# Attention in units of four heads: block transposes on VectorE, scores on four 32-row tiles, and the weights of six experts loaded late

## The chip, the cores and the metric

The kernel runs on one core of a Trainium2 chip. The metric is the device time of one execution in microseconds (us). It was taken several times for each kernel; a time is called fast when it is within 1.5% of the fastest of the same kernel. Only fast runs are compared, and all ratios are fast runs against fast runs of the kernel before, run in turn on the same chip.

Names used below: PE is TensorE, PEld its weight loads, DVE is VectorE, ACT is ScalarE, POOL is GpSimd, SP is SyncE (here it only issues DMAs). AV is the product of the attention weights with v, and the granted clock is the share of its full clock that TensorE was allowed. L307 is line 307 of the kernel in question, so line numbers differ between kernels.

## The reference

Attention for 4 batches, 8 heads, 768 positions and 64 dimensions, with a distance bias and a mask that keeps the first 8 positions and the 96 most recent ones. Its 3072 output rows (512 wide) then go through a mixture of 8 experts: the gate scores of all tokens are sorted, and tokens are handed out so that each expert gets exactly 384. Each expert is two matrix products with a ReLU between.

```python
def _attn_ref(q, k, v, n_global, n_local):          # q, k, v: (4, 8, 768, 64) fp32
    scores = np.matmul(q, k.transpose(0, 1, 3, 2)) / np.sqrt(D)
    is_global = pos[None, :] < n_global             # 8
    is_local = (rel >= 0) & (rel < n_local)         # 96
    ...
    scores = np.where(is_global | is_local, scores + bias[None], -1e9)
    a = softmax(scores)                             # cut
    return np.matmul(a, v)

def _moe_ref(x, w_gate, w1, w2):                    # x: (3072, 512), 8 experts, 1024 hidden
    order = np.argsort(-(x @ w_gate).flatten())
    ...                                             # greedy, at most 384 tokens each
    for e in range(E):
        out[assigned == e] = np.maximum(x[assigned == e] @ w1[e], 0.0) @ w2[e]
```

## The kernel before

The kernel has three stages, one after the other: attention, routing (which ends with the indices `idi`, saying which token goes to which expert), and the experts, which gather their rows from `x_tok` in DRAM by those indices.

Attention works on pairs of heads. q and k are loaded with six consecutive tokens to a partition, GpSimd reorders them, TensorE transposes them in blocks of 128, VectorE and ScalarE copy the results out. The scores of a pair take 14 matmuls of 64 rows (a head's 64 dimensions), two of them side by side in the array. The trace lists each fp32 score matmul as two records (28 a pair), here called half-passes.

```python
def reorder(n, dst, srcs):                                    # GpSimd
    nc.gpsimd.tensor_copy(out=dst.rearrange("p j t d -> p t j d"), in_=srcs[n % NR])

def kT(n, hf):                                                # TensorE: fp32 transposes of k
    pt = ps_t.tile([128, 3, 128], FP32, tag="pt")
    for jj in range(3):
        nc.tensor.transpose(pt[:, jj, :], kn[:, 3 * hf + jj, :, :].rearrange("p t d -> p (t d)"), ident)
    return pt
# ... kT_out: VectorE copies pt into kA.  qT, qT_out: the same for q, copied by ScalarE ...

def scores(n, g):
    kA, qTt = kAs[n % 2], qTs[n % 2]
    ps = ps_s.tile([128, 2, 512], FP32, tag="ps")
    for i in GROUPS[g]:
        _, o, w = POS[i]
        for t in range(2):                                    # two heads, two tiles of 64 rows
            r = slice(64 * t, 64 * t + 64)
            nc.tensor.matmul(ps[:, t, o : o + w], lhsT=kA[r, i, :], rhs=qTt[r, KT * i : KT * i + w],
                             start=True, stop=True)
    return ps

# per pair n, interleaved in one hand-ordered program (cut):
#   scores, expo (ACT), mask (DVE), attend = AV (PE), sums (PE), sums_out (DVE: LT),
#   tok (PE: transposes of the outputs, pk), tok_out (DVE: x, scaled by ri from LT)
```

The w1 of all experts and the w2 of two are loaded during attention. The w2 of the other six (6 pieces of 1 MB) go into memory that attention's buffers leave free, so they are issued when attention is nearly done, by GpSimd, which later issues the gathers as well (the source writes the last two after the first gathers, but in the built program all six stand ahead):

```python
w2_late = w2pool.tile([128, N_EXP - W2_EARLY, NFC, DM], BF16)          # W2_EARLY = 2
for e in range(W2_EARLY, N_EXP - 2):
    late_w2(e)                                                # nc.gpsimd.dma_start
# ... routing ...
def load_x(e):
    for t in range(TSLAB):
        nc.gpsimd.indirect_dma_start(out=xe, ..., in_=x_tok[:, :], in_offset=...idi...)   # gather
        # 4 PE transposes into pxe, one VectorE copy into xT
```

The softmax here doesn't subtract the row's maximum and nothing guards it: scores larger than these inputs give would overflow.

## Time and profile before

| before | |
|---|---|
| time | 321.07 us median of 3 (320.95 to 324.28; the result below counts a fourth) |
| span in the profile, granted clock | 321.0 us, 0.970 |
| busy: PE, DVE, ACT, POOL | 289.9, 155.8, 111.8, 124.1 us |
| attention ends (first filler matmul of routing; fillers only keep TensorE busy) | 174.96 us |
| expert indices ready, first gather issued | 206.42 us |
| first transposes of gathered rows | 211.27 us |
| first output matmuls of expert 0 | 228.67 us |

The windows table gives, for each stretch of the span, the busy time of each engine, then the granted clock of TensorE, the busy share of the DMA engines and GB/s. These are two of its rows for the kernel before:

```profile
core 0: us, PE busy (x) PEld busy (x) DVE busy (x) ACT busy (x) POOL busy (x), PEclk, DMA share, GB/s
...
60.00:80.00 20.00, 20.00 (x278) 15.47 (x278) 12.40 (x25) 9.06 (x14) 12.35 (x17) 1.00 1.08 242
...
220.00:240.00 20.00, 15.51 (x81) 8.30 (x81) 2.93 (x5) 6.24 (x14) 6.85 (x8) 0.83 0.22 74
```

In attention (here 60 to 80 us) PE is busy without a gap; in the other stretches from 20 to 160 it is busy for 19.4 to 20.0 of 20 us, and VectorE for 12.4 to 15.0. Attention is bound by TensorE. In the last row, at the start of the experts, PE has gaps and a lower clock.

The groups by line, with shapes kept apart, show what a removed or added piece costs: line, engine, operation, output and inputs, shape and count; then busy time and mean ns of one; then the idle time before it and what ended it.

```profile
L322 PE MATMUL ps<-qT,kA 64*128 64x215 f32 x320 | 43.7, 385 | 0.7 <-ACT qT L311 0.7
...
L337 DVE TENSOR_TENSOR P<-P,Wm 128x860 f32<-128x860 f32 x16 | 24.1, 1509 | 13.6 <-ACT P L330 13.6
...
L290 PE MATMUL pt<-ident,kn 128*128 128x128 f32 x96 | 15.3, 300 | 5.6 <-DMA kn<-in_k_dram 5.1 <-POOL kn L267 0.5
```

L322 are the scores, L290 the transposes of k (those of q look the same). L337 is the middle mask, whose mean of 1509 ns is high for its size: the other two masks take 1048. In the timeline it takes 1.05 to 1.06 us in nine pairs, and 1.36 to 2.88 in the seven in which a GpSimd reorder copy (L267) runs at the same time.

The timeline lists instructions by start and duration, neighbours of one kind merged. TensorE of the kernel before, one pair of heads from scores to scores:

```profile
66.59 1.07 PE L322 MATMUL ps<-qT,kA 64*128 64x215 f32 x12
...
70.29 0.87 PE L290 MATMUL pt<-ident,kn 128*128 128x128 f32 x6
...
72.93 0.87 PE L307 MATMUL pt<-ident,qn 128*128 128x128 f32 x6
...
76.60 1.07 PE L322 MATMUL ps<-qT,kA 64*128 64x215 f32 x12
```

The pair takes 76.60 - 66.59 = 10.01 us. The two rows with `pt` (0.87 us each; start to start with the next row 1.6 us together) are what the change takes off TensorE.

And the start of the experts, TensorE in the timeline of the kernel before:

```profile
211.27 0.61 PE L856 MATMUL pxe<-ident_bf,xe 128*128 128x128 bf16 x8 [0.44 <-DVE fc L832]
...
213.91 3.97 PE L870 MATMUL ph<-xT,w_all 128*128 128x384 bf16 x16 [0.15 <-DVE xT L857]
...
221.77 0.81 PE L870 MATMUL ph<-xT,w_all 128*128 128x384 bf16 x4 [2.70 <-issue]
225.30 2.72 PE L870 MATMUL ph<-xT,w_all 128*128 128x384 bf16 x8 [2.72 <-ACT hT L873]
...
228.67 6.03 PE L879 MATMUL po<-w_early,hT 128*128 128x512 bf16 x24
```

The same stretch of the timeline for GpSimd, which issues weights and gathers:

```profile
170.66 5.28 POOL L535 DMA_DIRECT2D w_late<-in_moe_w_dram  x6 [17.40 <-PE po L364]
206.42 1.08 POOL L850 DMA_INDIRECT xe<-x_tok,idi  x1 [30.49 <-DVE idi L704]
```

The six late pieces were issued at 170.66 and the first gather at 206.42, as soon as the indices were there. The rows came with hardly a wait. But expert 0's first products (32 matmuls, L870) took from 213.91 to 227.8, with two gaps of 2.7 us; the later experts need 5.4 us for the same 32.

### The profile page before, as it was taken

The numbers are of one execution on the slowest core, as the hardware profiler recorded it, in microseconds if no ns is written. First come the engines' busy times: TensorE is split into PE (matmuls) and PEld (weight loads), VectorE is DVE, ScalarE is ACT, GpSimd is POOL, SyncE is SP. The second block draws the span as 40 slices with busy tenths as digits, with TensorE's granted clock in tenths as the row PEclk, the third lists the DMA queues.
The fourth block names the chain that finished last, engine by engine and source line by source line (L and its number), as shares of the span: only waits on it lengthen the run. The fifth ranks groups of instructions, "written<-read, shape, count | busy, mean of one in ns | idle before, by whom it ended". The sixth has DMA issues, their size and how long they took to land. (4 is left out here: it accounts for less than half of the span.)

```text
span 321.0 us, 7142 instructions
## 1 busy us (share of the span) xinstructions
PE 289.9 (90%) x2918; PEld 191.8 (60%) x2918; DVE 155.8 (49%) x332; ACT 111.8 (35%) x193; POOL 124.1 (39%) x178
## 2 busy tenths in 40 slices
PE   3899999999999999999996888873999999999980
PEld 2577777777777777777774443331455555555530
DVE  2366658865567776777554566520123322422220
ACT  3474544434444344443440010001241243234310
POOL 5453554257753235421006000275246444312320
PEclk9999999999999999999999899979699999999996
DMA  8999978999699996985005999933123233102211
GB/s 152 266 276 230 261 182 196 257 189 266 166 228 266 202 267 138 224 178 104 3 2 64 209 214 207 201 108 98 33 100 134 62 115 132 67 33 98 100 66 41
DMA packets 58327, 49.25 MB, mean 153 GB/s; under 512 B 32944, under 2 KB 51888, under 8 KB 58288
## 3 DMA queue, kind: packets, MB, share of 16 engines
q0 software_dynamic: 15776, 26.22, 39.9%
q1 hardware_dynamic: 42512, 22.50, 27.0%
q8 instruction: 25, 0.41, 0.5%
q14 instruction: 14, 0.11, 0.1%
HBM read 56.05 MB, written 9.44 MB: 204 GB/s over the span
## 5 line engine op out<-in xcount | busy, mean ns | idle before, releaser
L330 ACT ACTIVATE P<-ps 128x860 f32<-128x860 f32 (+1 forms) x48 | 42.7, 890 | 64.9 <-PE ps L322 64.9
L873 ACT ACTIVATE hT<-ph 128x384 bf16<-128x384 f32 x64 | 30.8, 491 | 79.1 <-PE ph L870 71.9
L322 PE MATMUL ps<-qT,kA 64*128 64x215 f32 (+2 forms) x448 | 50.7, 352 | 0.7 <-ACT qT L311 0.7
L870 PE MATMUL ph<-xT,w_all 128*128 128x384 bf16 x256 | 45.9, 338 | 6.0 <-issue 3.1
L364 PE MATMUL po<-P,v 128*64 128x215 f32 (+6 forms) x576 | 47.5, 298 | 1.0 <-DVE P L344 1.0
L302 POOL COPY kA<-kA 128x56 f32<-128x56 f32 x16 | 16.2, 1015 | 74.2 <-PE po L364 38.8
L322 PEld LDWEIGHTS ps<-qT,kA 64*128 64x128 f32 x448 | 37.6, 191 | 11.3 <-issue 10.2
L850 POOL DMA_INDIRECT xe<-x_tok,idi x24 | 23.1, 963 | 53.5 <-DVE idi L704 30.5
L870 PEld LDWEIGHTS <-w_all 128*128 128x128 bf16 x256 | 25.7, 101 | 25.3 <-issue 9.2
L364 PEld LDWEIGHTS po<-P,v 128*64 128x64 f32 x576 | 31.4, 136 | 11.8 <-issue 7.4
L883 POOL DMA_INDIRECT out_dram<-ot,idi x24 | 23.6, 982 | 37.4 <-DVE ot L882 32.3
L344 DVE TENSOR_TENSOR P<-P,Wm 128x860 f32<-128x860 f32 (+1 forms) x32 | 33.5, 1048 | 2.6 <-ACT P L330 2.6
L879 PE MATMUL po<-w_late,hT 128*128 128x512 bf16 x144 | 32.9, 379 | 0.0
L857 DVE COPY xT<-pxe 128x512 bf16<-128x512 bf16 x24 | 9.5, 422 | 44.5 <-PE pxe L856 43.5
L882 DVE COPY ot<-po 128x512 f32<-128x512 f32 x24 | 16.6, 692 | 30.0 <-PE po L879 27.9
L337 DVE TENSOR_TENSOR P<-P,Wm 128x860 f32<-128x860 f32 x16 | 24.1, 1509 | 13.6 <-ACT P L330 13.6
L879 PEld LDWEIGHTS <-hT 128*128 128x128 bf16 x192 | 18.5, 99 | 20.0 <-issue 0.8
L395 PEld LDWEIGHTS pr<-P,onesx 128*32 128x32 f32 x768 | 24.6, 109 | 6.1 <-ACT qT L311 4.4
L395 PE MATMUL pr<-P,onesx 128*32 128x168 f32 (+11 forms) x768 | 27.6, 259 | 0.0
L295 DVE COPY kA<-pt 128x360 f32<-128x360 f32 x32 | 17.1, 534 | 18.6 <-PE pt L290 18.6
L573 PE MATMUL pw<-w_all,ident_bf 128*128 128x512 bf16 x51 | 20.0, 393 | 3.8 <-DVE x L435 1.8
L369 ACT COPY oT<-po 128x384 f32<-128x384 f32 x32 | 15.3, 479 | 21.5 <-PE po L364 21.4
(142 smaller groups left out, 304.2 us busy)
## 6 DMA issues: line engine op xcount, KB each, us to landing
w_all<-in_moe_w_dram POOLq DMA_DIRECT2D x16, 512.0 KB
w_late<-in_moe_w_dram POOLq DMA_DIRECT2D x6, 1024.0 KB
v<-in_v_dram SPq DMA_DIRECT2D x32, 180.0 KB, 4.1
kr<-in_k_dram SPq DMA_DIRECT2D x15, 384.0 KB, 6.9
qr<-in_q_dram SPq DMA_DIRECT2D x15, 384.0 KB, 6.6
x_tok<-x SPq DMA_DIRECT2D x16, 192.0 KB, 4.0
w_early<-in_moe_w_dram POOLq DMA_DIRECT2D x4, 512.0 KB
v<-in_v_dram SPq DMA_DIRECT2D x32, 14.0 KB
```

What stands on the lines that cost most here:

```text
L322: nc.tensor.matmul(ps[:, t, o : o + w], lhsT=kA[r, i, :], rhs=qTt[r, KT * i : KT * i + w], start=True, stop=True)
L330: nc.scalar.activation(P[:, :, 0 : GW[g]], ps[:, :, 0 : GW[g]], AF.Exp, scale=0.125)
L337: nc.vector.tensor_tensor(out=P[:, :, 0:430].rearrange("p t (o w) -> p t o w", o=2), in0=P[:, :, 0:430].rearrange("p t (o w) -> p t o w", ...
L344: nc.vector.tensor_tensor(out=P[:, :, 0 : GW[g]], in0=P[:, :, 0 : GW[g]], in1=Wm[:, h0 : h0 + 2, lo : lo + GW[g]], op=ALU.mult)
L364: nc.tensor.matmul(po[n][bk][64 * t : 64 * t + 64, a - QB * bk : z - QB * bk], lhsT=v7[:, t, i, :], rhs=P[:, t, o + a - q0 : o + z - q0], ...
L395: nc.tensor.matmul(o_, lhsT=l_, rhs=r_, start=first[gq], stop=True, skip_group_check=True)
L573: nc.tensor.matmul(pw, lhsT=ident_bf, rhs=w1_all[:, 0, 0, 0:512], start=True, stop=True)
L850: nc.gpsimd.indirect_dma_start(out=xe, out_offset=None, in_=x_tok[:, :], in_offset=bass.IndirectOffsetOnAxis(ap=idi[:, s : s + 1], axis=0),)
L870: nc.tensor.matmul(ph, lhsT=w1_all[:, e, kc, 128 * fc : 128 * fc + 128], rhs=xT_e[:, kc, :, :].rearrange("p t n -> p (t n)"), start=(kc == ...
L873: nc.scalar.activation(hT[:, fc, :], ph, AF.Relu)
L879: nc.tensor.matmul(po, lhsT=hT[:, fc, 128 * t : 128 * t + 128], rhs=w2_of(e)[:, fc, :], start=(fc == 0), stop=(fc == NFC - 1))
L883: s = nc.gpsimd.indirect_dma_start(out=out[:, :], out_offset=bass.IndirectOffsetOnAxis(ap=idi[:, TSLAB * e + t : TSLAB * e + t + 1], axis= ...
```

## The change

Attention works in units of four heads. Each of the 32-dimension halves of four heads fills the 128 partitions, so scores run on four tiles of 32 rows, and the products of the two halves are added in PSUM. The transposes of q and k move from TensorE to VectorE, which transposes blocks of 32 x 32. AV, sums and output transposes of a unit run one unit behind its scores. To make room, only two experts' weights are loaded early and twelve pieces of 1 MB late, and gathers are issued two experts ahead.

The intent: TensorE loses work, VectorE takes it over. The core of the diff:

```diff
-        qn = natp.tile([128, NBLK, 2, D_], FP32)
-        kn = natp.tile([128, NBLK, 2, D_], FP32)
+        qr = natp.tile([128, NJ, D_], FP32)                  # NJ = S_ // 32 = 24
+        kr = natp.tile([128, NJ, D_], FP32)
+        kTn = natp.tile([128, 2, NT * KT], FP32)
...
+        def load_u(u, dst, src):
+            b, hf = divmod(u, 2)
+            nc.sync.dma_start(dst.rearrange("p j d -> p (j d)"),
+                              src[b, 4 * hf : 4 * hf + 4].rearrange("a (c j) d -> (a c) (j d)", j=NJ))
-        def reorder(n, dst, srcs):
-            nc.gpsimd.tensor_copy(out=dst.rearrange("p j t d -> p t j d"), in_=srcs[n % NR])
...
+        def blocks(dst, src, g):
+            nc.vector.transpose(out=dst[:, g, 0:S_].rearrange("p (c j) -> p j c", j=NJ),
+                                in_=src[:, :, 32 * g : 32 * g + 32])
...
+        def kA_out(u):
...
+            nc.scalar.copy(out=kA[:, :, :, 8:128], in_=kTn.rearrange("p g (i k) -> p g i k", i=NT))
...
         for i in GROUPS[g]:
-                for t in range(2):
-                    r = slice(64 * t, 64 * t + 64)
-                    nc.tensor.matmul(ps[:, t, o : o + w], lhsT=kA[r, i, :], rhs=qTt[r, KT * i : KT * i + w],
-                                     start=True, stop=True)
+                for gd in range(2):
+                    for a in range(4):
+                        r = slice(32 * a, 32 * a + 32)
+                        nc.tensor.matmul(ps[a // 2][:, a % 2, o : o + w], lhsT=kA[r, gd, i, :],
+                                         rhs=qTt[r, gd, KT * i : KT * i + w],
+                                         start=(gd == 0), stop=(gd == 1), skip_group_check=True)
...
         with tc.manual_schedule():
+            load_u(0, kr, k)
+            load_u(0, qr, q)
...
+            kT(0)
+            load_u(1, kr, k)
...
+            for n in range(NB):                              # NB = 4
+                load_v(n)
+            for u in range(NU + 1):
+                A, Bp = 2 * (u - 1), 2 * (u - 1) + 1
...
+                if cur:
+                    ps = scores(u, 0)
+                    expo(u, 0, ps)
...
+                if nxt:
+                    kT(u + 1)
+                    if u + 2 < NU:
+                        load_u(u + 2, kr, k)
+                if cur:
+                    mask(2 * u, 0)
+                    mask(2 * u + 1, 0)
+                if prev:
+                    av(A)
...
+                    pr = sums(A)
+                if nxt:
+                    qT(u + 1, 0)
+                    kA_out(u + 1)
+                if prev:
+                    sums_out(A, pr)
+                weight_piece()
...
-    w2_late = w2pool.tile([128, N_EXP - W2_EARLY, NFC, DM], BF16)
+    w1_late = w2pool.tile([128, N_EXP - W_EARLY, NKC, F_DIM], BF16)                 # W_EARLY = 2
+    w2_late = w2pool.tile([128, N_EXP - W_EARLY, NFC, DM], BF16)
...
+    for _ in range(4):
+        late_weights()                                       # one 1 MB piece each
...
+            gather(0)
             load_x(0)
-            if first:
-                late_w2(N_EXP - 2)
-                late_w2(N_EXP - 1)
+            gather(1)
             for e in range(N_EXP):
+                if first:
+                    late_weights()
+                if e + 2 < N_EXP:
+                    gather(e + 2)
+                if first:
+                    late_weights()
```

A partition holds 24 consecutive tokens (`j`), so a transposed block is written with a step of 24 elements, 96 bytes. And the stage after attention is ordered by a scheduler, not by hand: the source writes four late pieces ahead of the gathers, but in the built program's GpSimd order nine stand there.

## The prediction

> **What bounds the kernel now.** The timeline shows three stages: attention to about 173 us, routing to 211, experts to the end. In the windows table, PE is busy 20.0 of 20 us in nearly every stretch from 20 to 160 us, VectorE only 12.4 to 15.0, ScalarE about 9; the DMA share is near 1 but PE hardly waits for it (waits view: 5 us for the first k tile). So attention is TensorE-bound, about 10.0 us per pair of heads. From start to start in the timeline, one pair costs: scores 2.9 us, q and k transposes 1.6 to 1.7, AV 2.75, sums and gates 2.0, token transposes 0.8.
>
> **Removed.** On PE: twelve fp32 transposes a pair (1.65 us x 16 = 26 us). Switches between kinds of matmul (0.2 to 0.28 us each) become fewer, since AV runs uncut and scores take four heads at a time. VectorE loses the kA copies (534 + 174 ns, twice a pair); ScalarE loses the qT copies (577 ns, twice a pair). GpSimd loses the reorder copies; I read these as the reason why the second mask takes 1.05 us in some pairs and up to 2.9 in others (mean 1.51).
>
> **Added.** Scores: twice the matmuls, at half the rows, four side by side. A half-pass of 215 columns now starts every 175 ns, two tiles 7 ns apart. The Trainium skill (TensorE: Matmul & The Clock Gate, Part 3) states that row tiles run together; I expect four within about 20 ns, so the score time per pair stays. PE per unit of four heads: 5.3 + 4.6 + 4.0 + 1.6 = 15.5 us, against 20.
>
> VectorE gets four transposes of 768 columns a unit. Their writes step 96 bytes. The skill (Advanced Engine Details and Errata, SBUF Cachelines) says a new 16-byte line per access costs; the only strided fp32 SBUF read here, the 384-element reduce (857 ns against an estimated 0.55 us), agrees. Estimate 1.56 us each (0.95 if free). VectorE per unit: masks 6.3 + transposes 6.2 + sums 2.0 + token copies 2.2 = 16.7 us, slightly over PE. So VectorE becomes the limit, at 17 to 17.7 us a unit. ScalarE adds about 1.9 us of kA copies a unit.
>
> Walking the program order with these durations: unit 0 ends near 25 us (larger loads, no AV to overlap), seven units of about 17.4, a last one of 11 with AV alone. Attention ends near 159 us: 15 us earlier. Free strides would give about 148.
>
> **Weights.** Before, 6 MB of late weights (206 GB/s in the DMA histogram) are in just before the token gathers are issued, 36 us after the last AV. Now the GpSimd order puts nine 1 MB pieces ahead of the gathers on the same queue. I expect them to drain 5 to 8 us after the indices are ready, so the first expert starts late, and cold. Against that, expert 0 now loses about 7 us in two unexplained 2.7 us PE gaps and a half-rate clock; some may go.
>
> **Prediction.** 321 - 15 + 6 - 3 = 309 us; 298 to 320. Faster 0.76, same 0.20, slower 0.04.
>
> **Right or wrong.** Groups by line: score matmuls still about 350 ns with starts 175 ns apart; VectorE block transposes 1.5 to 1.7 us; masks 1.05. Windows: VectorE above 90% in attention, PE below. Timeline: attention ends near 159 us; PE waits for gathered rows before expert 0. If transposes take 0.95 us, expect about 300. Wrong if four row tiles do not overlap (scores double: +20 us), if weight loads of 128 columns serialize, if single-buffered k, q or scores make PE wait for VectorE more than walked, or if late weights delay later experts too.

## The result

The changed kernel takes 338.44 us (median of 4, 337.55 to 340.35) against 321.01 (320.59 to 324.28) for the kernel before. The ratio is 1.0528 (95% interval 1.0444 to 1.0611): slower by 5%. Ratios here and below are the mean time of one kernel's fast runs over that of the other's of the same rounds, so not quite the ratio of the medians.

| from the profiles, us | before | after | what this step adds |
|---|---|---|---|
| attention ends | 174.96 | 178.90 | +3.9 |
| routing's last matmul (L830, after: L846) | 210.59 | 215.15 | +0.6 |
| first transposes of gathered rows | 211.27 | 230.04 | +14.2 |
| first output matmuls of expert 0 | 228.67 | 239.94 | -7.5 |
| end of the span | 321.0 | 335.7 | +3.4 |

So the saving that attention should have brought is not there, the rows of the first expert come late, and expert 0 itself is quicker. The windows table of the kernel after:

```profile
40.00:60.00 20.00, 14.15 (x247) 11.68 (x250) 17.90 (x21) 8.60 (x12) 0.00 (x0) 0.83 0.51 132
60.00:80.00 20.00, 18.40 (x368) 15.27 (x361) 19.13 (x25) 8.77 (x13) 1.98 (x7) 1.00 0.65 155
...
220.00:240.00 20.00, 9.79 (x57) 5.94 (x58) 1.78 (x5) 3.73 (x8) 9.42 (x10) 0.59 0.80 176
```

From 60 to 80 us the roles have changed: VectorE (third figure) is busy 19.1 of 20 us, PE 18.4; the next stretch has 19.2 and 17.1. From 40 to 60 PE has only 14 us of work: that is unit 1. From 220 to 240 it waits for rows. The groups of the kernel after:

```profile
L307 PE MATMUL ps<-qT,kA 32*128 32x215 f32 x640 | 43.9, 397 | 15.4 <-DVE qT L266 11.4 <-ACT P L321 3.3 <-DVE ident_bf L69 0.7
...
L266 DVE STREAM_TRANSPOSE kTn<-kr 128x768 f32<-128x768 f32 x16 | 31.9, 2098 | 12.5 <-DMA kr<-in_k_dram 12.5
...
L328 DVE TENSOR_TENSOR P<-P,Wm 128x860 f32<-128x860 f32 x16 | 16.3, 1061 | 1.6 <-ACT P L321 1.6
```

The score matmuls have doubled in number to 640 of this shape, and their summed busy time is the same as before (43.9 against 43.7 us), because busy time counts overlapping matmuls once. The middle mask fell from 1509 to 1061 ns. The 16 block transposes of k cost 2.10 us each and those of q 2.08, 64.8 us in all. TensorE in unit 2, scores and the output transposes of the unit before:

```profile
61.12 1.74 PE L307 MATMUL ps<-qT,kA 32*128 32x215 f32 x32
62.79 0.55 PE L419 MATMUL pk<-ident,oT 128*128 128x128 f32 x3
64.90 0.55 PE L419 MATMUL pk<-ident,oT 128*128 128x128 f32 x3 [1.56 <-DVE LT L399]
```

32 half-passes take 1.74 us, and all scores of a unit 5.4 (32, 32 and 48 of them), where two pairs took 6.1 before. In the third row PE waits 1.56 us for `LT`, a small VectorE transpose in the queue of the busy VectorE; such a wait is there in each of units 1 to 6 (1.56 to 7.66 us). Units start at 11.4, 27.5, 55.0, 72.8, 91.9, 111.9, 132.2, 149.9 us (from the first score matmuls of each), so unit 1 takes 27.5 us, the middle ones 17.8 to 20.3, the last 16.0. In the two longest, units 4 and 5, the second AV takes 4.2 us instead of the 2.5 of unit 2, at a granted clock of 0.59 (102.8 to 107.0 and 123.1 to 127.3 us), after PE had waited 2.2 and 2.4 us. Why the clock fell is not shown: a wait of 2.9 us in unit 3 was not followed by it here, but it was in the second profile of this kernel (r_after, below).

Unit 1 of the kernel after in the timeline of TensorE:

```profile
37.61 0.55 PE L419 MATMUL pk<-ident,oT 128*128 128x128 f32 x3
45.82 0.90 PE L419 MATMUL pk<-ident,oT 128*128 128x128 f32 x3 [7.66 <-DVE LT L399]
```

The same unit in the timeline of VectorE:

```profile
37.76 3.99 DVE L266 STREAM_TRANSPOSE kTn<-kr 128x768 f32<-128x768 f32 x2 [8.27 <-DMA kr<-in_k_dram]
...
45.37 0.40 DVE L399 STREAM_TRANSPOSE LT<-pr 128x192 f32<-128x192 f32 x1
```

And in the timeline of SyncE's queue, where a duration is that of the issue, not of the transfer:

```profile
21.57 5.20 SPq L260 DMA_DIRECT2D v<-in_v_dram  x1
...
28.75 2.33 SPq L260 DMA_DIRECT2D v<-in_v_dram  x1
...
33.02 0.36 SPq L250 DMA_DIRECT2D kr<-in_k_dram  x1
```

Read the last fence first. The load of k for unit 2 (`kr`) was issued only at 33.02, behind the loads of v for two more pairs, one of which stood in the queue for 5.20 us and one for 2.33. VectorE waited 8.27 us for that k and did nothing else in that time, so its transpose `LT` came at 45.37, and PE waited 7.66 us for `LT`. A wait put down to "DVE LT" is a wait for a DMA two steps back.

The start of the experts, TensorE in the timeline of the kernel after:

```profile
230.04 2.14 PE L878 MATMUL pxe<-ident_bf,xe 128*128 128x128 bf16 x16 [14.64 <-DMA xe<-x_tok,idi]
...
239.94 2.32 PE L906 MATMUL po<-w_early,hT 128*128 128x512 bf16 x10
```

And GpSimd in the same timeline:

```profile
178.80 6.54 POOL L548 DMA_DIRECT2D w_late<-in_moe_w_dram  x8 [71.05 <-DVE x L427]
188.87 0.76 POOL L548 DMA_DIRECT2D w_late<-in_moe_w_dram  x1 [3.54 <-DMA w_late<-in_moe_w_dram]
210.96 1.08 POOL L866 DMA_INDIRECT xe<-x_tok,idi  x1 [21.33 <-DVE idi L720]
```

GpSimd could issue the first eight of the nine pieces only at 178.80, when VectorE had read the last output of attention (`x L427`), 8 us later than the six of the kernel before. The first gather was issued at 210.96, right after the indices, but its rows arrived only when the nine pieces were through, at 230: PE waited 14.64 us.

### The profile page after: what moved, and what is told of

It is laid out like the page before. It is cut to its first block, busy times and chain, and to the rows that moved or that the text cites. A ratio compares the mean times of both kernels' runs of the same rounds, so it can differ in the third digit from the quotient of the medians.

```text
span 335.7 us, 7401 instructions
## 1 busy us (share of the span) xinstructions
PE 268.1 (80%) x3174; PEld 182.4 (54%) x3174; DVE 188.0 (56%) x300; ACT 108.3 (32%) x177; POOL 80.7 (24%) x126
## 3 DMA queue, kind: packets, MB, share of 16 engines
q1 hardware_dynamic: 36848, 22.50, 25.6%
## 5 line engine op out<-in xcount | busy, mean ns | idle before, releaser
L307 PE MATMUL ps<-qT,kA 32*128 32x215 f32 (+2 forms) x896 | 52.3, 368 | 15.4 <-DVE qT L266 11.4
L307 PEld LDWEIGHTS ps<-qT,kA 32*128 32x128 f32 x896 | 43.7, 207 | 21.9 <-ACT kA L277 11.4
L355 PEld LDWEIGHTS po<-P,v 128*64 128x64 f32 x576 | 37.4, 148 | 9.2 <-issue 3.4
L266 DVE STREAM_TRANSPOSE kTn<-kr 128x768 f32<-128x768 f32 x16 | 31.9, 2098 | 12.5 <-DMA kr<-in_k_dram 12.5
L897 PE MATMUL ph<-xT,w_late 128*128 128x384 bf16 x192 | 32.7, 326 | 1.4 <-ACT hT L900 1.0
L419 PE MATMUL pk<-ident,oT 128*128 128x128 f32 x96 | 17.6, 295 | 19.9 <-DVE LT L399 18.3
L266 DVE STREAM_TRANSPOSE qT<-qr 128x768 f32<-128x768 f32 x16 | 32.9, 2080 | 0.0
L548 POOL DMA_DIRECT2D w_late<-in_moe_w_dram x12 | 10.1, 865 | 74.6 <-DVE x L427 71.1
L386 PE MATMUL pr<-P,onesx 128*32 128x192 f32 (+11 forms) x768 | 27.6, 259 | 0.0
L897 PEld LDWEIGHTS <-w_late 128*128 128x128 bf16 x192 | 18.8, 98 | 14.9 <-issue 2.1
```

Of the source, the lines that this page charges most:

```text
L266: nc.vector.transpose(out=dst[:, g, 0:S_].rearrange("p (c j) -> p j c", j=NJ), in_=src[:, :, 32 * g : 32 * g + 32])
L307: nc.tensor.matmul(ps[a // 2][:, a % 2, o : o + w], lhsT=kA[r, gd, i, :], rhs=qTt[r, gd, KT * i : KT * i + w], start=(gd == 0), stop=(gd = ...
L355: nc.tensor.matmul(po[n][bk][64 * t : 64 * t + 64, a - QB * bk : z - QB * bk], lhsT=v7[:, t, i, :], rhs=P[:, t, o + a - q0 : o + z - q0], ...
L386: nc.tensor.matmul(o_, lhsT=l_, rhs=r_, start=first[gq], stop=True, skip_group_check=True)
L419: nc.tensor.transpose(pk[:, bb, :], oTs[n][:, 3 * hf + bb].rearrange("c g r -> c (g r)"), ident)
L897: nc.tensor.matmul(ph, lhsT=w1_of(e)[:, kc, 128 * fc : 128 * fc + 128], rhs=xT_e[:, kc, :, :].rearrange("p t n -> p (t n)"), start=(kc == ...
```

## The experiments

Three theories, which were formed from the two traces, and their rivals:

- **W**, the weights: the rows wait because nine pieces stand ahead of the gathers in the same queue. Rival: gathers are slow by themselves, or the DMA is too loaded for the order to matter.
- **S**, the order of SyncE's queue: unit 1 is long because k for unit 2 is issued behind loads of v. Rival: unit 1 is short of VectorE time or of DMA rate, whatever the order.
- **T**, the transposes: the units of 17.8 to 20.3 us are long because each block transpose takes 2.09 us rather than 1.56, and this comes from the write step of 96 bytes. Rival: 2.09 us is what this instruction costs at this size, or VectorE isn't what holds the units up.

The first four ran on one chip together (before: 323.43 us), so that each undoes one thing, and the fourth all three.

### e1_order: weights of experts 4 to 7 allocated after routing

```diff
-    w1_late = w2pool.tile([128, N_EXP - W_EARLY, NKC, F_DIM], BF16)
+    W_MID = 4
+    w1_late = w2pool.tile([128, W_MID - W_EARLY, NKC, F_DIM], BF16)
...
     routing(False)
+    w3pool = ctx.enter_context(tc.tile_pool(name="w3pool", bufs=1))
...                                          # the pieces of experts W_MID to 7 get their tiles here
     experts(True)
```

> The changed kernel with one thing undone: of the late weights only four 1 MB pieces (experts 2 and 3) stand ahead of the token gathers; the other eight lie in memory that routing uses, so they can't be issued before it ends. Theory W (the 14.6 us in which PE waits for gathered rows is the queue behind nine weight pieces): the wait falls to 3 us or less, attention and routing unchanged, total 338.4 - 12 = about 326 us (323 to 329). Rival (gathers are slow whenever weights move, or the later experts then wait for their own weights): total within 4 us of 338, with PE idle moved into experts 2 to 5.

Measured: 1.0220 (1.0152 to 1.0287), 329.57 us. GpSimd's timeline has four pieces ahead of the gathers (issued at 174.49, 4.3 us earlier than in the kernel after, as they wait for other buffers), and TensorE's timeline of e1_order has the rows early:

```profile
215.51 0.61 PE L888 MATMUL pxe<-ident_bf,xe 128*128 128x128 bf16 x8 [0.44 <-DVE fc L858]
218.39 0.67 PE L888 MATMUL pxe<-ident_bf,xe 128*128 128x128 bf16 x8 [2.27 <-DMA xe<-x_tok,idi]
```

The wait for rows is 2.3 us instead of 14.6. W holds: about 10 us of the loss (1.0528 to 1.0220 of 323) is the place of the weights. It was a little less than expected. The remaining weights now move among the experts' scatters: VectorE waits 27.3 us for output buffers to come free, and PE has new waits of 1 to 2.5 us between experts. That this makes up the difference was not tested.

### e2_vlast: v of pairs 2 and 3 loaded behind k and q of unit 2

```diff
-            for n in range(NB):
-                load_v(n)
+            load_v(0)
+            load_v(1)
...                                                      # in unit 0, after load_u(2, qr, q):
+                if u == 0:
+                    load_v(2)
+                    load_v(3)
```

> The changed kernel with the v loads of pairs 2 and 3 moved behind the k and q loads of unit 2. Theory S (VectorE waits 8.3 us for the k tile of unit 2 because its load was issued only at 33 us, behind v loads in the same in-order queue): the load is issued before 26 us, the wait falls below 3 us, attention ends 5 to 9 us earlier, total about 331 (329 to 334). Rival (the first 38 us are bound by DMA bandwidth, about 190 GB/s moved): the issue moves but the landing does not, total within 2 us of 338.

Measured: 1.0144 (1.0081 to 1.0208), 328.19 us. VectorE's waits for k in the waits view (us in all, times, longest), first the kernel after, then e2_vlast:

```profile
DVE kTn L266 <- DMA kr<-in_k_dram: 12.5, 3, 8.3
...
DVE kTn L266 <- DMA kr<-in_k_dram: 4.0, 2, 3.6
```

Unit 1 takes 18.5 us instead of 27.5, attention ends at 169.7 instead of 178.9, and the wait for rows is no shorter (16.15 us). S holds: 9.2 us of attention's length was the order of issues in one queue.

### e3_contig: every 32nd token in a partition, so that transposes write side by side

```diff
-            nc.sync.dma_start(dst.rearrange("p j d -> p (j d)"),
-                              src[b, 4 * hf : 4 * hf + 4].rearrange("a (c j) d -> (a c) (j d)", j=NJ))
+            for a in range(4):
+                nc.sync.dma_start(dst[32 * a : 32 * a + 32, :, :],
+                                  src[b, 4 * hf + a].rearrange("(j c) d -> c j d", j=NJ))
...
-            nc.vector.transpose(out=dst[:, g, 0:S_].rearrange("p (c j) -> p j c", j=NJ),
+            nc.vector.transpose(out=dst[:, g, 0:S_].rearrange("p (j c) -> p j c", j=NJ),
```

> The changed kernel with q and k loaded so that a partition holds every 32nd token (256-byte pieces, four loads a tensor): the VectorE block transposes then write their results side by side instead of 96 bytes apart. Theory D (VectorE is the limit of the attention stage, and the stride of the writes makes one transpose 2.09 us): a transpose takes 0.9 to 1.0 us, VectorE is no longer above 90% busy, a unit takes 15.6 to 16.5 us instead of 17.8 to 20.2, total about 321 (315 to 327). Rival 1 (the transpose of fp32 is slow whatever the stride): 2.0 us or more, total unchanged or worse. Rival 2 (TensorE's own work, four row tiles, sets the unit): transposes get short, the unit stays above 17.5 us. Rival 3 (the 256-byte pieces make the loads late): transposes short, VectorE waits for k and q.

Measured: 1.0333 (1.0250 to 1.0416), 334.28 us, a gain of only 6 us. The transposes of k in the groups of e3_contig:

```profile
L267 DVE STREAM_TRANSPOSE kTn<-kr 128x768 f32<-128x768 f32 x16 | 14.7, 955 | 24.0 <-DMA kr<-in_k_dram 24.0
```

The transposes halved to 0.96 us, and where nothing else is in the way the units take 16.0 us (67.6 to 83.7 to 99.6), the PE time that was predicted. But the loads, now in pieces of 256 bytes instead of 6 KB, came late: VectorE waits 24.0 us for k and 6.3 for q (12.5 and 0 in the kernel after), and PE has two gaps of 8.3 and 8.1 us. On the page of this run, the queue of these loads moves the same 22.5 MB in 84,720 packets instead of 36,848 and takes 38.3% of the DMA engines' span instead of 25.6%, which fits. The experiment is not a clean test of T: it exchanged one cost for another.

### e4_all: the three together

The edits of e1, e2 and e3 in one kernel.

> The three edits together (few weights ahead of the gathers, v loads of pairs 2 and 3 later, side-by-side writes). If the three causes are separate and add: 338 - 12 - 7 - 17 = about 302 us (296 to 310), faster than the kernel before (321). If only one of them matters, close to the best single one of the three.

Measured: 0.9872 (0.9812 to 0.9932), 319.47 us: 1.3% faster than the kernel before, and far from the 302 expected. Attention ended at 171.5, no earlier than with e2 alone, with PE gaps of 4.1 and 7.8 us. Before them the transposes of k waited for loads, 7.1 us for k and 6.5 us for what the trace puts down to a load of v in the same queue. The gains add up only if the loads keep up, and in this kernel they didn't.

### e5_contig_wrong: transposes side by side with the 6 KB loads

The result is wrong (relative error 0.143): the loads stay as in the kernel after, only the write pattern changes, so tokens land in the wrong order. This separates the write step from the load size.

```diff
-            nc.vector.transpose(out=dst[:, g, 0:S_].rearrange("p (c j) -> p j c", j=NJ),
+            nc.vector.transpose(out=dst[:, g, 0:S_].rearrange("p (j c) -> p j c", j=NJ),
```

> Wrong result on purpose: the changed kernel with its 6 KB loads kept and only the write pattern of the block transposes made side by side (so the tokens stand in a permuted order). It parts the two effects that the 256-byte loads of the side-by-side run mixed. If those loads cost what the short transposes gained (that run won only 6 us of an expected 17, with two waits of 8 us for k): transposes 0.96 us, a unit 16.0 us, one wait for k (unit 2, about 8 us) instead of two, total 338.4 - 15 = about 323 on the first chip's scale (ratio to before 1.005 to 1.02). If TensorE's own work is the limit that ate the gain: ratio stays near 1.033.

Measured, on another chip (before: 322.72 us): 0.9845 (0.9797 to 0.9893), 317.16 us, better than expected. Attention ended at 158.3, 20.6 us earlier than in the kernel after. A row of the windows of e5_contig_wrong, columns as above:

```profile
60.00:80.00 20.00, 19.97 (x418) 17.22 (x418) 15.93 (x27) 10.56 (x16) 2.55 (x7) 1.00 0.88 186
```

Its transposes of k, in the groups by line:

```profile
L266 DVE STREAM_TRANSPOSE kTn<-kr 128x768 f32<-128x768 f32 x16 | 14.7, 954 | 15.3 <-DMA kr<-in_k_dram 15.3
```

PE is back at 20 of 20 us, VectorE at 15.9; from unit 2 on, units take 15.9 to 16.0 us. In unit 1 VectorE still waits 9.22 us for k and PE 4.76, and the wait for rows stays at 15.17. T holds, and it is the largest of the three. Of the 20.6 us, 15.1 lie in units 2 to 7, 3.5 in unit 0 and 2.1 in unit 1. With quicker transposes in unit 0 the whole queue moves on earlier, so k of unit 2 was issued at 27.40 rather than 33.02, but still behind v: unit 1 takes 25.5 us here, and 18.5 in e2. So this gain and the 9.2 us of e2 are mostly different ones; no run has just these two edits, so their sum isn't measured.

### e8_strides: sixteen extra transposes with eight write steps

```diff
+            for st in probe:                             # 1, 2, 3, 4, 6, 8, 12, 24 elements
+                for _ in range(2):
+                    nc.vector.transpose(out=probe[st].rearrange("p (a c b) -> p a b c", b=st, c=32),
+                                        in_=qr[:, :, 0:32].rearrange("p (a b) d -> p a b d", b=st))
```

> The changed kernel with sixteen extra block transposes at the end of attention, into scratch tiles that nothing reads: same input, 768 columns, writes 4, 8, 12, 16, 24, 32, 48 and 96 bytes apart, each twice. The skill's 16-byte lines (a line must be hit twice for full rate): about 0.96 us at 4 and 8 bytes, slow (about 2.1 us) from 16 bytes on, one plateau. A rival in which the cost grows with the stride: a slope between 8 and 96 bytes. Total about 25 us above the changed kernel, which means nothing.

Each transpose has 128 x 768 fp32 elements; durations of the two from the trace, in the order of the program:

| write step, bytes | 4 | 8 | 12 | 16 | 24 | 32 | 48 | 96 |
|---|---|---|---|---|---|---|---|---|
| ns | 968, 968 | 939, 951 | 1158, 1216 | 1486, 1528 | 1508, 1529 | 1540, 1555 | 1482, 1510 | 2055, 2086 |

The last of these in VectorE's timeline of e8_strides:

```profile
201.98 2.09 DVE L539 STREAM_TRANSPOSE probe<-qr 128x768 f32<-128x768 f32 x1
```

Two steps, not one. Up to 8 bytes the step is free, from 16 to 48 it costs half as much again, and 96 bytes cost more than double. The Trainium skill (Advanced Engine Details and Errata, SBUF Cachelines) states 16-byte lines and that at least two hits on a line are needed for full speed. The first step agrees: free at 8 bytes (two hits), at its full size from 16. The second step the page does not have. So the prediction's 1.56 us was right for steps of 16 to 48 bytes, and the kernel uses 96.

### e6_paced3: e4 with paced weights

The rival of "256-byte loads are too slow" was that the loads only collide with the early weights, whose issue is not paced. Against e4: the early weights (three experts, two pieces a unit) wait for the unit's output by a small GpSimd copy; six pieces stand ahead of the gathers; eight output buffers instead of four; one constant is copied by VectorE instead of GpSimd.

```diff
-                weight_piece()
+                if prev:
+                    nc.gpsimd.tensor_copy(out=pace_t[:, u : u + 1], in_=oTs[A][:, 0, 0, 0:1])
+                    for _ in range(2):
+                        weight_piece()
```

> An attempt at a better version, a correct one: the three edits together, plus three experts' weights early instead of two, their twelve pieces paced by a tiny GpSimd copy of each unit's output (before, GpSimd stood 46 us waiting for one VectorE constant and then sent the pieces in a burst that met the k loads), six pieces ahead of the gathers, the last four behind, and eight output buffers. If the burst caused the 8 us wait for k in unit 5, and scatters behind weights cost the experts some 8 us: ratio to before 0.94 to 0.965 (303 to 312 us where before is 323). Rival (the 256-byte loads alone make k late): the wait stays, ratio above 0.97.

Measured: 0.9992 (0.9917 to 1.0068), 326.52 us; four of its six runs fell into the slow state, the profiled one too, so this is a weak result, and the waits of its profile (VectorE 17.3 us for q, 8.7 for k) can't be compared with fast runs. Pacing did not help: a miss. Nor does it settle the rival, since the third early expert came with it, and e10 will show what that costs.

### e7_actperm3: 6 KB loads, transposes side by side, and ScalarE puts the tokens in order

```diff
-            nc.vector.transpose(out=dst[:, g, 0:S_].rearrange("p (c j) -> p j c", j=NJ),     # write step 96 bytes
-                                in_=src[:, :, 32 * g : 32 * g + 32])
+            nc.vector.transpose(out=dst[:, g, :, 0:32], in_=src[:, :, 32 * g : 32 * g + 32])
...
+        def q_out(u):
+            nc.scalar.copy(out=qTs[u].rearrange("p g (c j) -> p g c j", j=NJ),
+                           in_=qTn.rearrange("p g j c -> p g c j"))
```

The rest is as in e6_paced3.

> As the paced version, but with the 6 KB loads of the change kept: VectorE writes its transposes side by side, and the copies that ScalarE makes anyway (k) or newly (q, 1536 elements a unit) put the tokens in order, reading 128 or 144 bytes apart. If ScalarE pays little for strided reads (its earlier strided copies took 577 against 479 ns): kA copies below 2.5 us together, q copy below 2.2 us, ScalarE below 85% busy, no waits for k after unit 2, ratio 0.92 to 0.95. If a strided read costs ScalarE as much as a strided write costs VectorE (2.7 ns an element): 4.5 us each, ScalarE near 90% busy, unit above 17 us, ratio above 0.96.

Measured: 0.9748 (0.9688 to 0.9807), 314.69 us, a correct result, and 1.9 to 3.1% faster than the kernel before. Attention ended at 166.3. The strided pass went to ScalarE, where the q copy takes 2898 ns and the two k copies 1745 each, and units took 17.2 to 17.5 us. Against one k copy of 1593 ns in the kernel after, that is 4.8 us more a unit, no less than the 4.5 (4 x 1.13) that strided writes cost VectorE; but ScalarE had the room (busy 14.8 to 15.9 of 20 us with it).

### e9_pairs2: pairs of tokens, so that both sides are cheap

e8 says that a write step of 8 bytes is free. If a partition holds every 32nd pair of tokens, loads come in 512-byte pieces and the transpose writes with a step of 8 bytes. Together with e2's order of v, one paced early piece a unit, six pieces ahead of the gathers, then one piece for each expert, held back until that expert's hidden layer exists. Eight output buffers and the constant on VectorE are as in e6_paced3.

```diff
+            for a in range(4):
+                nc.sync.dma_start(dst[32 * a : 32 * a + 32, :, :].rearrange("p (r b) d -> p r (b d)", b=2),
+                                  src[b, 4 * hf + a].rearrange("(r c b) d -> c r (b d)", c=32, b=2))
...
+            nc.vector.transpose(out=dst[:, g, 0:S_].rearrange("p (r c b) -> p r b c", c=32, b=2),
+                                in_=src[:, :, 32 * g : 32 * g + 32].rearrange("p (r b) d -> p r b d", b=2))
...
+                if first and lates:
+                    nc.gpsimd.tensor_copy(out=lates[0][0][:, 0, 0:1], in_=hT[:, 0, 0:1])
+                    late_weights()
```

> A correct version built from the stride sweep: a partition holds every 32nd pair of tokens, so the loads have 512-byte pieces and the transposes write 8 bytes apart (0.95 us in the sweep). With it: v loads of pairs 2 and 3 later, one early weight piece a unit, six pieces ahead of the gathers, then one piece an expert, each held back by a tiny write. If write stride, load order and queue order are the three causes, and 256-byte pieces were what made k late in the paced run: transposes below 1.0 us, units of 16.0 us after the first two, no wait for k or q above 3 us, attention ends near 154, experts within 96 us of the first row transposed; ratio to before 0.93 to 0.95 (300 to 307 us where before is 322). If DMA is short even so: waits for k or q remain, ratio above 0.97.

Measured, on a third chip (before: 312.58 us): 0.9310 (0.9287 to 0.9333), 290.74 us, correct. A row of its windows, columns as above:

```profile
60.00:80.00 20.00, 19.65 (x368) 16.40 (x370) 18.01 (x32) 10.48 (x15) 2.69 (x5) 1.00 1.18 201
```

Its transposes of k, in the groups by line:

```profile
L268 DVE STREAM_TRANSPOSE kTn<-kr 128x768 f32<-128x768 f32 x16 | 14.7, 958 | 7.3 <-DMA kr<-in_k_dram 7.3
```

PE is busy 19.65 of 20 us again, attention ends at 154.2 (174.96 in the profile of the kernel before, on another chip), and the rows cause no wait above 1.4 us; one wait of VectorE for k, 5.0 us, is longer than the 3 expected. The change's own idea was sound; its three losses could be repaired. How much of this kernel's gain each of its several edits brings was not separated.

### e10_pairs3: the same with three experts early

```diff
-W_EARLY = 2
+W_EARLY = 3
...                                  # one piece in even units, two in odd ones; six still ahead of the gathers
+                    for _ in range(2 if u % 2 else 1):
```

> As the pairs version, but three experts early (1.5 pieces a unit) and four pieces left for the expert stage. If attention has DMA to spare at 512-byte pieces: 2 to 4 us faster than the pairs version, through the experts. If attention is then short of DMA: waits for k or q come back (units above 16.5 us) and it is slower than the pairs version.

Measured beside e9: 0.9661 (0.9615 to 0.9707), 302.87 us. Attention ended at 164.8, with PE gaps of 2.7 and 3.2 us at 89 and 126 us, and VectorE waited for loads and once for a store of outputs. Half a piece more in each unit comes with 10.6 us more of attention: in these two runs attention had no room for more weights.

### e11_before_gather: the kernel before with the gathers two experts ahead

The kernel before loses time in expert 0 (15 us from first product to first output, where 5.9 would do). A rival reason for the kernel after's quicker expert 0 was its earlier gathers. This is the only part of the change here, put into the kernel before.

```diff
+            gather(0)
             load_x(0)
+            gather(1)
...
+                if e + 2 < N_EXP:
+                    gather(e + 2)
```

> The kernel before with one part of the change alone: the token gathers are issued two experts ahead of their use. If the 7 us that expert 0 lost before (13.9 us of matmuls where later experts take 5.4) came from the order of gathers and transposes, it goes and the ratio to before is 0.975 to 0.985. If not (the scheduler had already put the gathers far ahead): within 0.5% of before.

Measured beside e9: 0.9955 (0.9925 to 0.9986), 311.84 us. In its timeline of TensorE, expert 0 loses nothing:

```profile
214.13 5.36 PE L881 MATMUL ph<-xT,w_all 128*128 128x384 bf16 x32
...
219.99 5.13 PE L890 MATMUL po<-w_early,hT 128*128 128x512 bf16 x23
```

That looked like a proof, but the unchanged kernel before took 312.58 us on this chip, 8 to 11 us less than on the others. So the loss was most likely absent there already (no profile of the unchanged kernel was taken on this chip), and this run can't show that the order of gathers removes it.

### r_before, r_after, r_pairs2: the three kernels side by side on a fourth chip

No edits: the kernel before, the kernel after and e9_pairs2 once more. What was open: does the loss in expert 0 follow the kernel or the chip?

> The kernel before, unchanged, for a second profile. If the loss in expert 0 belongs to the chip or session: either about 321 us with a first expert of 17 us from its first transpose to its first output matmul, or about 312 us with one of 8 us, and time and profile agree. If the loss is no part of the 9 us between jobs: 312 us with the gaps, or 321 without.

> The changed kernel, unchanged, on the same chip as r_before. If r_before shows no loss in expert 0: ratio to before about 1.07 to 1.08 (338 to 312); if it shows it: 1.05 again. In both cases transposes 2.09 us and 14 to 16 us of PE waiting for gathered rows.

> The pairs version again, beside both on one chip: 289 to 292 us; ratio to before 0.93 if before has no loss in expert 0 here, 0.90 if it has.

Measured (before of the same rounds: 322.49 us): r_before 0.9985 (0.9941 to 1.0029), r_after 1.0496 (1.0457 to 1.0535) at 339.38 us, r_pairs2 0.9365 (0.9317 to 0.9412) at 301.92 us. Expert 0 in the timeline of TensorE of r_pairs2:

```profile
192.40 2.11 PE L911 MATMUL ph<-xT,w_early 128*128 128x384 bf16 x12
...
201.81 1.44 PE L911 MATMUL ph<-xT,w_early 128*128 128x384 bf16 x4 [2.02 <-issue]
...
206.45 5.61 PE L923 MATMUL po<-w_early,hT 128*128 128x512 bf16 x23 [0.22 <-issue]
```

The same kernel that needed 5.9 us from first product to first output of expert 0 in e9 needs 14.0 here; r_before needs 15.2. r_after needs 7.8 (235.38 to 243.19).

r_after ended attention at 182.3 us, 3.4 later than the first profile of that kernel (unit 1 takes 30.4 us there), so single profiles carry a spread of this size; the 9.2 and 20.6 us of e2 and e5 are well above it.

So the loss of 8 to 9 us comes and goes with the chip or the session (not separated), hits the kernel before and the repaired one alike, and is not seen in any profile of the kernel after. r_pairs2 gathers two experts ahead and has the loss, so the order of gathers is not its cure. Why it is there, and why the kernel after escapes it, stays open. r_pairs2 missed its expectation of 289 to 292 us, and with the loss in both kernels the ratio was 0.937 and not 0.90. The ratio of e9's edits hardly depends on it (0.931 and 0.937). The ratio of the kernel after might: it was never run on a chip without the loss, and there it would probably look worse.

## Why the prediction was wrong

The prediction said 309 us (298 to 320), faster with 0.76. The kernel took 338.

What was right: the kernel before was bound by TensorE in attention. The four row tiles run together: the Trainium skill (TensorE: Matmul & The Clock Gate, Part 3) says so, and the trace agrees (112 half-passes of a unit in 5.4 us, 0.05 us each, against 0.11 with two tiles: 28 in 3.1 us). PE needs 16 us for a unit where nothing holds it (predicted: 15.5), as e3 and e5 show. The middle mask fell to 1.06 us without the reorder copies, VectorE became the limit, and nine pieces stood ahead of the gathers.

What failed, step by step:

1. **"Estimate 1.56 us each (0.95 if free)."** The mechanism was right, the size was off: 2.09 us, because the write step of 96 bytes lies beyond a second, larger step that the one strided instruction of the kernel before (a reduce) could not show. Four of them a unit are 2.1 us more than predicted, on the engine that had just become the limit. Against the predicted 17.4 us a unit, units 2 to 6 take 17.8 to 20.3. e5 shows the whole price of strided writes in attention: 20.6 us, where the prediction put it at 11 (159 to 148).
2. **"unit 0 ends near 25 us ..., seven units of about 17.4".** The walk looked at engines, not at the queue that issues loads. Unit 1 took 27.5 us because k of unit 2 was issued behind v. e2 gets 9.2 us back by moving two lines. The prediction's own sum, 25 + 7 x 17.4 + 11 = 158, against the trace of the kernel after: unit 0 ends at 27.5 (+2.5), unit 1 takes 27.5 (+10.1), units 2 to 7 take 110.9 together (+6.5), and the rest 13.0 (+2.0). That is the 21 us up to the measured 178.9. Half of the +6.5, 3.3 us, is what AV lost at the lower clock in units 4 and 5. Unit 1 is the largest piece.
3. **"drain 5 to 8 us after the indices are ready".** The rows came 19.1 us after the indices (210.96 to 230.04; 4.9 us in the kernel before), and PE waited 14.6 of them. The order was foreseen, the length mis-sized. Three more pieces than before at the 206 GB/s that the prediction names are 15 us by themselves (an estimate, 3 x 1.05 MB), so 5 to 8 us needed an earlier start. The prediction counts 36 us from the last AV to the gathers, and in the kernel before the pieces were issued right after it. Here their memory came free only at 178.80, when VectorE had read the last outputs, 6 us after the last AV, and they took until 230; routing covers only 32 us of that. e1 gets about 10 us back.
4. **"- 3" for expert 0.** It was 7.5 less, so this step erred to the other side; r_pairs2 and r_before, beside e9, show that the loss in expert 0 depends on the chip or the session.

In the prediction's sum, "- 15" became +3.9 and "+ 6" became +14.2, and these two are the error; the rest nearly cancels.

## What to carry to other kernels

When work moves to an engine that then becomes the limit, measure the moved instruction with its real access pattern and size before trusting the sum, since a factor of two in one instruction was the largest loss here; and change the layout of the load so that the write step is small while the load's pieces stay large enough. Walk the issuing queues of DMAs as carefully as the engines: a load behind others in the same queue, or a gather behind a megabyte of weights, costs as much as slow arithmetic. When several losses are found, test them one by one and together, since their gains need not add: e4 was predicted at 302 us and took 319.

## What the Trainium skill lacked or had wrong

- Advanced Engine Details and Errata, SBUF Cachelines: the rule (16-byte lines, two hits) agrees with the first step, but the page gives no size and has no second step. Here 768 columns of fp32 took 0.94 to 0.97 us at write steps of 4 and 8 bytes, 1.48 to 1.56 at 16 to 48, and 2.06 to 2.09 at 96.
- VectorE: DVE Perf Modes, Rules for kernel authors, calls the VectorE transpose the fastest for 32 x 32 blocks, without a word on the output's step: the same instruction took 0.96 or 2.09 us here, depending on it.
- DMA: Bandwidth & Descriptors, Two DMAs through the same engine are not ordered, says that descriptors within one queue of one DMA engine start in order. The trace fits that, but the page does not warn what that means for urgent small transfers: gathers issued at 210.96 landed near 230 behind nine pieces of 1 MB.
- No page that was read tells of the loss of 8 to 9 us at the start of the experts, present on some chips or in some sessions and absent in another (before: 322.5 and 312.6 us).
